# Two changes of order in a tuned attention and MoE kernel: when one block is transposed, and when the last chunk's own scores are made

## Chip, cores and metric

One NeuronCore of a Trainium2 chip. The metric is the device time of one launch, in microseconds (us), lower is better. The kernel is bound by TensorE (PE) almost throughout, so that this study is about a few us out of 1188.

## The reference, cut to what matters

```python
scores = (1.0 / S) * np.matmul(z, z.transpose(0, 2, 1))   # z: (8, 3008, 64)
attn   = np.maximum(scores, 0.0) ** 2
x      = u * np.matmul(attn, v)                           # u, v: (8, 3008, 256)
h      = x.reshape(-1, 256) @ w_in                        # (256, 2048)
out    = (h * (1.0 / (1.0 + np.exp(-1.702 * h)))) @ w_out # (2048, 256)
```

The scores are symmetric: block (i, c) is the transpose of block (c, i). The kernel makes most blocks only once and lets the DMA engines transpose ("turn") them for the other use.

## The kernel before

A batch of 3008 rows has six chunks of up to 512 rows. `attend(b, i)` multiplies chunk i's squared scores with v, in 47 or so steps ("slots"). A "unit" (i, jp) is a pair of 128-row blocks of scores; ScalarE rectifies it and VectorE squares it into a tile `a`. In the first batch, blocks are turned in the order of a list:

```python
ORDER0 = [(0, 1), (0, 2), (1, 2), (0, 3), (1, 3), (0, 4), (2, 3), (1, 4), (2, 4), (3, 4)]

def turn_unit(b, i, jp, a):            # two of these make one block (i, jp // 2)
    ...
    sp.dma_start_transpose(TT[b, i, cj][:, k0:k0 + 2]..., a...)
```

Block (2, 3) is chunk 2's, turned for chunk 3. All turning goes through SyncE's one queue, in program order. Chunk 4 of the first batch then reads all blocks for one half of the channels (`c`), then for the other:

```python
elif i == full(b):                     # chunk 4, all batches but the last
    order = [[(c, FULL, j)] for c in cs for j in js]
    ...
else:                                  # two 64-row tiles at a time, swapped at half of the chunk
    order = [[(0, TOP, j), (1, LOW, j)] for j in js] + [half] + [[(1, TOP, j), (0, LOW, j)] for j in js]
```

At half of such a chunk the row tiles swap their PSUM banks; the first matmul after it waits for a GpSimd instruction that waits for the last one before it (`post` and `behind`, line 86: "the handshake"). At which slot new scores are made is a schedule. That of the last batch:

```python
SCHED_LAST = SCHED | {3: {n: 1 for n in (14, 34)} | {NJ: 2}, 4: {NJ: 2}, 5: {}}   # NJ = 24
```

So the last two units, chunk 5's own, (5,10) and (5,11), are made in slot 24 of chunk 4, and chunk 5's very first step reads their tile `al`, most of which is made from (5,10) by two DMA transposes (line 277).

## Time and profile before

| | before |
|---|---|
| median of the first comparison, 6 executions | 1188.24 us (1187.31 to 1188.84) |
| span of the profiled execution, TensorE busy | 1186.5 us, 1176.8 us |
| wait at 54.14 us, turned block (2,3), first batch | 1.84 us |
| wait at 1092.77 us, block `al`, last batch | 1.83 us |

TensorE's timeline of the kernel before has the two waits in brackets (start, duration, engine, line, operation, what ended the idle time):

```profile
55.98 0.82 PE L358 MATMUL o<-tt,V 64*128 64x512 f16 x6 [1.84 <-DMA tt<-a]
...
1094.60 0.37 PE L358 MATMUL o<-al,V 64*128 64x448 f16 x2 [1.83 <-DMA al<-a]
```

The page's row for the matmuls that read turned blocks (busy us, mean ns | idle before, releaser) has no other wait:

```profile
L358 PE MATMUL o<-tt,V 64*128 64x512 f16 (+1 forms) x1510 | 232.1, 377 | 1.8 <-DMA tt<-a 1.8
```

The handshake at half of chunk 4 of the last batch, in the timeline of weight loads:

```profile
1087.62 0.76 PEld L358 LDWEIGHTS <-V 64*128 64x128 f16 x10 [0.17 <-POOLq L86]
```

### The profile page before, as it was taken

What the parts mean: (1) busy time and instruction counts of PE and PEld (TensorE: products, weight loads), DVE (VectorE), ACT (ScalarE), POOL (GpSimd) and SP (SyncE); (2) the same over time, 40 slices, a digit from 0 to 9 for tenths busy, and PEclk for the clock granted to TensorE, in tenths of its full rate; (3) what the DMA queues carried; (4) which work ended last, traced back from release to release, by engine and by line L of the source; (5) the groups of instructions that cost most, each with busy time, mean ns of one, the idle gap of its engine ahead of it and who ended that gap; (6) DMA issues with size and microseconds to landing.
All of it is one profiled execution on the core that took longest, in us unless ns stands there. A gap on an engine that the chain in (4) does not pass through costs nothing.

```text
span 1186.5 us, 27918 instructions
## 1 busy us (share of the span) xinstructions
PE 1176.8 (99%) x11526; PEld 699.6 (59%) x11526; DVE 837.7 (71%) x1441; ACT 819.3 (69%) x997; POOL 226.6 (19%) x319
## 2 busy tenths in 40 slices
PE   9999999999999999999999999999999999999998
PEld 3446764467644676447754478544784457844577
DVE  6688865877758776587775877658786487763776
ACT  7778864688646887478764787657866578672785
POOL 5243101231012310133101430014200241001000
PEclk9999999999999999999999999999999999999999
DMA  9998677866787677855789457895558875694012
GB/s 218 162 146 134 124 146 133 85 110 135 141 135 84 108 151 144 134 78 95 157 146 133 78 94 153 158 115 96 114 126 167 109 97 105 143 163 90 1 37 73
DMA packets 378880, 142.88 MB, mean 120 GB/s; under 512 B 320032, under 2 KB 372640, under 8 KB 378752
## 3 DMA queue, kind: packets, MB, share of 16 engines
q1 hardware_dynamic: 320464, 99.39, 46.3%
q0 software_dynamic: 56768, 40.39, 23.5%
q8 instruction: 90, 1.47, 0.5%
q10 hardware_dynamic: 1520, 1.31, 0.3%
q14 instruction: 38, 0.31, 0.1%
HBM read 60.29 MB, written 24.64 MB: 72 GB/s over the span
## 4 chain that ended last, share of the span: by engine, by line
PE 96%; ACT 1%; DMA 1%; issue 1%; DVE 1%; SPq 0%; DVEq 0%; ACTq 0%
PE o L358 39%; PE hg L399 27%; PE st L518 24%; PE sc L235 5%; ACT rl L256 1%; DMA tt<-a 1%; PE yp L493 1%; DMA al<-a 0%; PE w L99 0%; DVE a L270 0%; ACT ZT L143 0%; SPq L277 0%; DVE ut L202 0%; ACT gf L407 0%; DVE WT L446 0%
## 5 line engine op out<-in xcount | busy, mean ns | idle before, releaser
L407 ACT ACTIVATE gf<-hg 128x1024 f32<-128x1024 f32 (+1 forms) x384 | 385.5, 1004 | 143.7 <-PE hg L399 121.4
L256 ACT ACTIVATE rl<-sc 128x1024 f16<-128x1024 f32 (+1 forms) x301 | 287.7, 993 | 153.7 <-PE sc L235 108.4
L358 PEld LDWEIGHTS <-V 64*128 64x128 f16 (+1 forms) x4052 | 218.0, 95 | 257.9 <-issue 16.3
L399 PE MATMUL hg<-xt,W 128*128 128x512 f16 (+1 forms) x1408 | 354.6, 374 | 0.0
L411 DVE TENSOR_SCALAR gt<-gf 128x1024 f16<-128x1024 f32 (+1 forms) x320 | 222.9, 697 | 137.2 <-ACT gf L407 134.5
L358 PE MATMUL o<-a,V 64*128 64x512 f16 (+3 forms) x2240 | 296.1, 368 | 0.2 <-DVE a L270 0.2
L270 DVE TENSOR_TENSOR a<-rl 128x1024 f16<-128x1024 f16 (+1 forms) x266 | 178.5, 675 | 123.3 <-ACT rl L256 122.6
L195 POOL DMA_DIRECT2D uq<-in_u_dram x188 | 127.8, 687 | 692.0 <-PE sc L235 456.4
L358 PE MATMUL o<-tt,V 64*128 64x512 f16 (+1 forms) x1510 | 232.1, 377 | 1.8 <-DMA tt<-a 1.8
L399 PEld LDWEIGHTS <-W 128*128 128x128 f16 x1536 | 139.3, 98 | 119.2 <-issue 2.6
L518 PEld LDWEIGHTS <-gt 128*128 128x128 f16 x2944 | 177.1, 98 | 32.2
L518 PEld LDWEIGHTS <-s 128*128 128x128 f16 x2208 | 133.7, 98 | 25.6 <-issue 0.5
L235 PE MATMUL sc<-ZT 64*128 64x512 f16 (+3 forms) x688 | 114.6, 356 | 0.7 <-ACT ZT L143 0.4
L518 PE MATMUL st<-WT,gt 128*128 128x128 f16 x1472 | 97.8, 219 | 0.0
L518 PE MATMUL st<-WT,s 128*128 128x128 f16 x1472 | 96.6, 219 | 0.2 <-ACT uP L530 0.2
L518 PE MATMUL st<-W,gt 128*128 128x128 f16 x1472 | 96.6, 219 | 0.0
L536 DVE SCALAR_TENSOR_TENSOR y<-st,uP 128x256 f32<-128x256 f32 (+1 forms) x144 | 57.9, 409 | 28.3 <-ACT uP L530 19.9
L530 ACT ACTIVATE uP<-st 128x256 f32<-128x256 f32 (+1 forms) x144 | 53.0, 368 | 31.5 <-DVE y L536 16.2
L375 DVE TENSOR_TENSOR xt<-o,ut 128x512 f16<-128x512 f32 x80 | 51.4, 684 | 27.6 <-PE o L358 27.6
L409 ACT ACTIVATE gt<-gf 128x1024 f16<-128x1024 f32 (+1 forms) x64 | 65.9, 1030 | 2.1
L474 DVE TENSOR_TENSOR s<-s,gt 128x1024 f16<-128x1024 f16 (+1 forms) x96 | 64.4, 671 | 1.1
L472 DVE TENSOR_TENSOR s<-gt 128x1024 f16<-128x1024 f16 (+1 forms) x96 | 64.8, 675 | 0.0
(53 smaller groups left out, 600.2 us busy)
## 6 DMA issues: line engine op xcount, KB each, us to landing
out_dram<-y SPq DMA_DIRECT2D x40, 512.0 KB, 3.6
uq<-in_u_dram POOLq DMA_DIRECT2D x156, 128.0 KB, 3.7
V<-in_v_dram POOLq DMA_DIRECT2D x35, 256.0 KB, 6.4
tt<-a SPq DMA_TRANSPOSE x232, 3.9
uq<-in_u_dram POOLq DMA_DIRECT2D x32, 112.0 KB, 4.6
out_dram<-y SPq DMA_DIRECT2D x7, 384.0 KB, 3.1
vst<-in_v_dram SPq DMA_DIRECT2D x3, 512.0 KB, 5.9
zst<-in_z_dram POOLq DMA_DIRECT2D x7, 192.0 KB, 8.4
```

The costliest lines, as they stand in the source:

```text
L195: eng.dma_start(uq[k * QW:(k + 1) * QW, :n // QW].rearrange("t q c k -> t q (c k)"), src[:, :, cs])
L235: pe.matmul(sc[:, r, :q1 - q0], zt[h, 2 * kp + r, :], zt[h].rearrange("d n p -> d (n p)")[:, q0:q1], start=True, stop=True,)
L256: act.activation(rl[:, :, :n], sc[:, :, :n], AF.Relu, scale=csc)
L270: dve.tensor_tensor(a[:, :, :n], rl[:, :, :n], rl[:, :, :n], ALU.mult)
L358: ins = pe.matmul(acc[c][:, :n], V16[b][h, j].rearrange("p (c k) -> p k c", k=NCC)[:, c], weights(b, i, j)[h], start=(k, m) == first[c], s ...
L399: pe.matmul(hg[:, e, :n], W1[:, c, ff * P:(ff + 1) * P], XT[b, i][:, c, :n], start=(c == 0), stop=(c == NCC - 1),)
L407: act.activation(gf[:, :, :n], hg[:, :, :n], AF.Gelu_apprx_sigmoid, scale=1.0 / FSC)
L409: act.activation(g, gf[:, :, :n], AF.Copy, scale=FSC)
L411: dve.tensor_scalar(g, gf[:, :, :n], FSC, None, ALU.mult)
L472: dve.tensor_tensor(s_, a21, a22, ALU.add)
L474: dve.tensor_tensor(s_, ST[b, k, "S1", h], a11, ALU.subtract)
L518: pe.matmul(bank[:, m, :], lhs()[:, f, m, :], right[:, ff, :], start=name in ("P1", "P2", "P5") and m == 0 and ff == 0, stop=ff == NFF // ...
```

## The change

Its intent is to take away both waits: (2,3) is turned one place earlier, and chunk 5's own units are made 22 slots earlier.

```diff
-    ORDER0 = [(0, 1), (0, 2), (1, 2), (0, 3), (1, 3), (0, 4), (2, 3), (1, 4), (2, 4), (3, 4)]
+    ORDER0 = [(0, 1), (0, 2), (1, 2), (0, 3), (1, 3), (2, 3), (0, 4), (1, 4), (2, 4), (3, 4)]
-    SCHED_LAST = SCHED | {3: {n: 1 for n in (14, 34)} | {NJ: 2}, 4: {NJ: 2}, 5: {}}
+    SCHED_LAST = SCHED | {3: {n: 1 for n in (14, 34)} | {NJ: 2}, 4: {2: 2}, 5: {}}
```

Below, "part A" is the order and "part B" the slot.

## The prediction

> **What bounds the kernel now.** I read the page first. Its engine row and the head of its chain of work say that TensorE sets the time nearly everywhere:
>
> ```profile
> PE 1176.8 (99%) x11526; PEld 699.6 (59%) x11526; DVE 837.7 (71%) x1441; ACT 819.3 (69%) x997; POOL 226.6 (19%) x319
> ...
> PE 96%; ACT 1%; DMA 1%; issue 1%; DVE 1%; SPq 0%; DVEq 0%; ACTq 0%
> ```
>
> Only 1186.5 - 1176.8 = 9.7 us of the span are without a matmul in the array, and part of that is the start and the last store. The change adds and removes no instruction, so all it can win lies in these 9.7 us. The second view is therefore TensorE's list of waits (who was waited for: total us, times, longest us):
>
> ```profile
> PE o L358 <- DMA tt<-a: 1.8, 1, 1.8
> PE o L358 <- DMA al<-a: 1.8, 1, 1.8
> PE w L99 <- DVE nil L75: 1.2, 1, 1.2
> ```
>
> Two single waits of 1.8 us are in reach: one for a transposed block `tt`, one for the last chunk's own block `al`. The timeline places them: 54.14 us (first batch, chunk 3) and 1092.77 us (last batch, first matmul of chunk 5). Everything between runs on TensorE without another wait over 0.2 us.
>
> The chain of work around the first one:
>
> ```profile
> 47.23 0.69 DVE a L270 x2
> 47.92 8.02 DMA tt<-a
> 55.94 0.04 issue
> 55.98 0.82 PE o L358 x6
> ```
>
> The transpose issued at 47.92 needed 8.02 us to land. The DVE row ahead of it is a coincidence: the program order shows that this is the second transpose of block (2,3), chunk 2 for chunk 3. Its data were squared in chunk 1's last slots, done at about 37.3 us (the second of two 0.69 us squares at 35.70 and 36.62). What held it is SyncE's own queue, which issues one transpose behind the other from 24.94 to 65.3 us with no pause over 0.15 us. Read one by one, its landings are: (1,3) 42.0 and 45.8, (0,4) 48.2 and 49.8, (2,3) 50.9 and 55.9, (1,4) 57.5 and 59.1, (2,4) 61.7 and 62.4, (3,4) 69.3 and 71.5 us.
>
> The chain around the second wait:
>
> ```profile
> 1087.51 0.21 PE sc L235 x2
> 1087.72 0.02 issue
> 1087.74 0.93 ACT rl L256
> ...
> 1089.51 1.18 SPq L277
> 1090.69 0.05 issue
> 1090.74 3.72 DMA al<-a
> 1094.46 0.14 issue
> 1094.60 0.66 PE o L358 x3
> ```
>
> This is latency, not load: scores at 1087.5, rectified, squared, two transposes, landing at 1094.46, while ScalarE had been idle for 7.26 us before it.
>
> **What the Trainium skill says.** "TensorE: Matmul & The Clock Gate", section "Back-to-back issue gap", gives N/2.4 + 2.5 ns between warm matmuls, 216 ns for N=512; here the pairs on two row tiles start at 1086.486, 1086.702 and 1086.918, so 0.216 us apart, while each is drawn 0.376 us long. A gap read between bars thus understates a stall. "TensorEngine Tiling (Array Packing)", "Gotcha 1: PSUM Pressure", says row tiles cannot access one PSUM bank at the same time and software has to synchronize; the kernel does this at half of a chunk with a GpSimd semaphore instruction, visible as a PEld wait at L86. "DMA: Bandwidth & Descriptors", "Queues, rings and completion order", says each DMA engine goes round-robin between queue rows by packets; from 66 to 70 us the software queue had 1462 packets and the hardware queue 1468, so it agrees. "Perfetto Trace Analysis", "DMA Instruction — HWDGE (DVE, Sync)", says that the reported span of such an instruction leaves out the movement; here issues of 1.2 to 5.3 us landed 3.2 to 11.3 us after their start.
>
> **Part A, the order of turning.** The two transposes of (2,3) change places with the two of (0,4); the order of all engines else is unchanged. Data of (2,3) are ready (37.3) before the earlier pair was issued (38.90), so nothing new holds the queue. (2,3) should land at about 48.2 and 49.8, and TensorE wants it at 54. The wait ends with 4 us to spare. What it cost: the last matmul before it started at 53.784 (448 columns, 0.19 us pitch), so the next was due at 53.975 and came at 55.979: 2.00 us, not 1.84. (0,4) now lands at 50.9 and 55.9; chunk 4 first reads it at 65.92 - 2.0 = 63.9. The buffers that (0,4) frees are next written some 10 us later; the program order moves that semaphore wait to squares at about 58 us. Both harmless.
>
> What is not free is the next deadline. Block (3,4), the last of the queue for chunk 4, landed at 71.51. Chunk 4's step 16 reads it, the third matmul of this row, so at 72.40 + 2 x 0.216 = 72.83:
>
> ```profile
> 72.40 0.81 PE L358 MATMUL o<-tt,V 128*128 128x512 f16 x3
> ```
>
> With TensorE 2.0 us earlier it wants (3,4) at 70.83. The DMA share in these stretches (window, its length, then busy time by engine; the last two columns are clock and DMA share with GB/s) is over one all the way:
>
> ```profile
> 38.00:54.00 16.00, 16.00 (x152) 7.25 (x147) 12.04 (x20) 13.72 (x15) 3.40 (x6) 1.00 1.22 138
> 54.00:56.00 2.00, 0.16 (x4) 0.02 (x3) 1.33 (x3) 1.01 (x2) 0.00 (x0) 1.00 1.14 146
> 56.00:73.00 17.00, 17.00 (x119) 8.43 (x119) 10.28 (x17) 13.47 (x15) 4.78 (x6) 1.00 1.35 192
> ```
>
> So the queue is bound by throughput and will not follow TensorE. If (3,4) lands where it did, a new wait of 71.51 + 0.04 - 70.83 = 0.72 us appears. GpSimd's weight loads and the next batch's z load start 2.0 us earlier too, as they wait for the half of chunk 3 (58.67 before); these are in front of (3,4) in both kernels, so finishing them earlier may bring it forward, by up to about 1 us as I judge it. I take a new wait of 0.4 us, between 0 and 0.8. Part A: 2.0 - 0.4 = 1.6 us.
>
> **Part B, the own units of chunk 5.** Four score matmuls move from slot 24 of chunk 4 to slot 2, about 1082.2 us. PSUM is free (last rectification ended at 1080.5), ScalarE idle, VectorE busy with the two gates until 1083.7; then square, transposes from about 1084.5 and, at the 3.7 to 4.0 us that the old ones took to land, data by about 1089. Needed at 1092.9. Without the wait: last matmul 1092.386, next due 1092.60, came at 1094.595, so 1.99 us.
>
> But slot 24 is where TensorE waits for the GpSimd handshake, and the moved matmuls covered it. Last matmul of the first half: start 1087.137, end 1087.513; GpSimd answers at 1087.555; TensorE goes on at 1087.627. With nothing in between it was due at 1087.349. So 0.28 us of it comes into the open. The 0.27 us of scores are paid in slot 2 instead. Part B: 1.99 - 0.28 = 1.71 us.
>
> **Sum.** 1.6 + 1.7 = 3.3 us. From the first wait on TensorE is the bound, so the shift should reach the end: 1187.97 - 3.3 = 1184.7 us, a ratio of 1.003.
>
> **Rivals.** (1) The queue keeps (3,4) back for the whole 0.72 us or, with loads mixing differently, longer, up to eating all of part A: for it speaks the DMA share over one, against it that loads ahead of it finish earlier. Time 1185.0 to 1186.3. (2) Waits vanish and nothing takes their place, the handshake being hidden by weight loads pulled ahead: 1187.97 - 4.0 = 1184.0. Against it: the weight load itself waits for the handshake, 0.17 us in the old trace even with cover. (3) VectorE and ScalarE, nearly on the path at 91 to 102 us (their rows are in the chain there), take back some of it: but that stretch starts from a TensorE score at 90.83 us and should shift as a whole; I give at most 0.3 us.
>
> **Range and chances.** All rivals lie between 1184.0 and 1186.3; three runs of before spread over 0.8 us. I take 1183.9 to 1186.0. Two per cent are 23.8 us, more than all idle time of TensorE, so faster by that is excluded; slower by that would need a stall that the program order doesn't show.
>
> **What would show it.** Right: no TensorE wait for `tt` near 54 us, none for `al` near 1090; (2,3) landed before 51 us; a short wait for `tt` near 71 us; a PEld wait at L86 near 1085 us of about 0.25 us where it was 0.17. Wrong: a first (2,3) transpose that starts after 40 us, a `tt` wait over 1 us at 71, a TensorE matmul count busy for longer than 1176.8 us by more than 1 us, or another wait in chunk 5 of the first batch that takes back what chunk 3 won.

## The result and the profile after

Ratios are the mean time of one kernel's runs over that of the other's of the same rounds, so not quite the ratio of the medians.

| | before | after |
|---|---|---|
| first comparison, median | 1188.24 us | 1185.74 us |
| lowest and highest of 6 | 1187.31, 1188.84 | 1184.62, 1191.08 |
| ratio, 95% interval | | 0.9988 (0.9968 to 1.0009) |
| span of the profiled execution | 1186.5 us | 1187.0 us |

The median fell by 2.5 us, but the ratio says only 1.4 us, because two of six executions took 1188.79 and 1191.08 us. By luck the profile is of the first of these, 4 us over the fastest. It shows what went wrong there. Its list of TensorE's waits, and the page's row:

```profile
PE o L358 <- DMA tt<-a: 3.6, 2, 3.1
```

```profile
L358 PE MATMUL o<-tt,V 64*128 64x512 f16 (+1 forms) x1510 | 232.3, 377 | 3.8 <-DMA tt<-a 3.6
```

The wait for `al` is gone. The wait for a turned block has not gone but moved, and grown from 1.8 to 3.6 us in two pieces. TensorE's timeline places them:

```profile
69.95 0.61 PE L358 MATMUL o<-tt,V 128*128 128x512 f16 x2 [0.54 <-DMA tt<-a]
...
77.60 0.38 PE L358 MATMUL o<-tt,V 128*128 128x512 f16 x1 [3.10 <-DMA tt<-a]
```

There is none at 54 us: (2,3) landed at 50.9 and 53.1 us, and the matmul that waited before has no bracket:

```profile
54.13 0.81 PE L358 MATMUL o<-tt,V 64*128 64x512 f16 x6
```

Block (2,4) landed at 69.9 instead of 62.4 us, and (4,5), the last of the queue, at 77.56 instead of 73.28 us. The chain of that execution at the second piece:

```profile
71.09 6.47 DMA tt<-a
77.56 0.04 issue
77.60 0.38 PE o L358
```

But this execution's queue was already late before the change could act. Up to (1,3) both kernels issue the same transposes in the same order, and the second transpose of (1,3) landed at 49.25 us here, at 45.84 us in the profile of before. So the DMA engines don't take the same time in two executions, and one profile of each kernel doesn't say what the order does.

In the last batch the profile answers without doubt. The two transposes of `al` go out at 1086.95, and the matmul that reads it follows its predecessor without a wait; the handshake, with nothing to cover it, shows 0.61 us of idle weight loading in place of 0.17:

```profile
1086.95 2.46 SPq L277 DMA_TRANSPOSE al<-a  x2
...
1095.06 0.35 PE L358 MATMUL o<-al,V 64*128 64x448 f16 x2
```

```profile
1090.08 4.86 PEld L358 LDWEIGHTS <-V 64*128 64x128 f16 x48 [0.61 <-POOLq L86]
```

The 0.61 us counts from the end of a weight load. What TensorE lost is read from starts: the last matmul of the first half began at 1089.589, the next was due 0.212 later, at 1089.80, and began at 1090.082: 0.28 us.

Because the instructions of TensorE are the same in all these kernels from the first batch's end to the last batch, whole stretches can be compared by start times of the same matmul. From the 10500th to the 10700th matmul record (last batch, chunk 4 into 5) the kernel before took 31.74 us and the changed one 30.01 us. Part B is worth 1.73 us here. The experiments below repeat this: the stretch took 30.01 us in every one of the fourteen profiles that have part B, and 31.74 to 33.60 us in the five that have the old slot (before, e1, g3, h1, h4).

### The profile page after: what moved, and what is told of

Its sections match the earlier page's. It is cut to its first block, busy times and chain, and to the rows that moved or that the text cites. A ratio compares the mean times of both kernels' runs of the same rounds, so it can differ in the third digit from the quotient of the medians.

```text
span 1187.0 us, 27920 instructions
## 1 busy us (share of the span) xinstructions
PE 1177.2 (99%) x11526; PEld 698.5 (59%) x11526; DVE 837.1 (71%) x1441; ACT 819.8 (69%) x997; POOL 226.0 (19%) x319
## 4 chain that ended last, share of the span: by engine, by line
PE 97%; ACT 1%; DVE 1%; DMA 1%; issue 0%; DVEq 0%; ACTq 0%; POOLq 0%
PE o L358 39%; PE hg L399 27%; PE st L518 24%; PE sc L235 6%; PE yp L493 1%; DMA tt<-a 1%; ACT rl L256 1%; PE w L99 0%; ACT gf L407 0%; DVE a L270 0%; DVE ut L202 0%; ACT ZT L143 0%; PE zp L135 0%; DVE zst L128 0%; DVE WT L446 0%
## 5 line engine op out<-in xcount | busy, mean ns | idle before, releaser
L530 ACT ACTIVATE uP<-st 128x256 f32<-128x256 f32 (+1 forms) x144 | 53.1, 368 | 31.7 <-DVE y L536 15.6
```

## The experiments

Two theories after the result. **C**: the moved wait is the change's doing, TensorE comes 2 us sooner to the last turned blocks while the next batch's z load is under way. **L**: the turning queue is late by itself in some executions, and either order pays for it somewhere. Five groups followed, eighteen kernels, each group on one chip with the kernel before in the same rounds. All gave correct results.

### Each part alone, the change again, and the z load held

`e1_order_only` has the first line of the diff alone, `e2_slot_only` the second alone, `e3_both_again` is the change. `e4_hold_z` is the change with one line more, which makes GpSimd read block (4,5) before it issues the second half of the next batch's z load:

```diff
+            if b == 1 and n0: pool.tensor_copy(const.tile([P, 1], F16, name="hold2"), TT[0, NCH - 2, NCH - 1][:, 2, 0, :1])
```

> The first part alone: (2,3) turned in front of (0,4); the last batch as before. Theory C (collision): the wait of 2.0 us at 54 us goes, but from 69 to 77 us TensorE waits for the last turned blocks (3,4) or (4,5), because it reaches them 2 us sooner while the second half of the next batch's z load shares the DMA engines with them; loss there 0 to 5 us, different from execution to execution, so the mean is within 1 us of before and the times spread by over 3 us. Rival P (as predicted): one new wait of at most 0.8 us, 1.2 to 2.0 us faster than before, spread under 2 us. In both the wait for the last chunk's own block near 1092 us stays at 1.8 us.

> The second part alone: own units of chunk 5 in slot 2 of chunk 4; the first batch as before. Both theories: no wait near 1093 us, 0.28 us lost at the handshake in slot 24, so 1.7 us faster than before (1.4 to 2.0), with the spread of before (about 1.5 us). The wait of 1.8 us near 54 us stays. If the second part were the cause of the wide spread, the times here would spread by over 4 us.

> The change again, unaltered, for a second profile and five more times. Theory C: times spread by over 3 us again, some at 1184.6 and some over 1187; in the profile the waits near 70 to 77 us add up to the profiled time less 1184.3. Rival Q (the first profile was an outlier of the measurement): times within 1.5 us of 1185.

> The change, and in the first batch GpSimd reads one column of block (4,5) before it issues the second half of the next batch's z load, so that this load cannot be under way while the last turned blocks land. Theory C: no wait of over 1 us at 74 us, mean 1184.3 to 1185.3, about 3.3 us faster than before, spread under 2 us. Rival L (the hardware queue is late by itself in some executions, whatever the z load does): spread over 3 us as with the change, and waits for turned blocks of 1 to 5 us near 70 to 77 us in slow executions.

| | median us | all executions | ratio to before (1187.40) |
|---|---|---|---|
| e1_order_only | 1187.42 | 1186.77 to 1188.69 | 1.0000 (0.9988 to 1.0012) |
| e2_slot_only | 1185.76 | 1185.20 to 1186.10, one 1189.34 | 0.9989 (0.9977 to 1.0001) |
| e3_both_again | 1185.51 | 1185.09 to 1185.56 | 0.9980 (0.9968 to 0.9992) |
| e4_hold_z | 1186.96 | 1184.64 to 1192.72, three over 1187.9 | 1.0008 (0.9988 to 1.0028) |

The order alone wins nothing that shows: its interval is 1.4 us wide to each side. The slot alone wins 1.64 us in the median, and both together 1.89 us. The profile of the slot alone says why. It has the old order, and the list of TensorE's waits begins

```profile
PE w L99 <- DVE nil L75: 1.2, 1, 1.2
PE sc L235 <- ACT ZT L143: 0.3, 1, 0.3
```

with no wait for a turned block at all: (2,3) landed at 47.86 us and was due at 54.5. In the profile of the order alone the only wait over 1.2 us is that for `al`:

```profile
PE o L358 <- DMA al<-a: 1.9, 1, 1.9
```

So the 2.0 us at 54 us in the first profile were one execution's, not the kernel's. Theory C fails as the general cause: both e1 and e3 run the new order without a wait in chunk 4, and the five executions of e3 lie within 0.5 us, where C expected over 3. e4 missed its expectation: its profiled execution was a fast one without waits, but three of its six were slow, and none of these was profiled. Holding the z load does not tame the spread, and whether it makes it worse is open.

### Chunk 4 relaxed, and a queue made late on purpose

`g1_pairs_both` is the change with chunk 4 of the first batch read block by block for both channel halves, which moves the first use of the last blocks back, by 8 us as the expectation has it (in g1's profile (3,4) is first read at 80.9 us and (4,5) at 85.2, which is 9.5 and 11.2 us later than half by half); `g2_pairs_slot_only` the same with the old order.

```diff
-            order = [[(c, FULL, j)] for c in cs for j in js]
+            order = [[(c, FULL, j)] for j in js for c in cs] if b == 0 else [[(c, FULL, j)] for c in cs for j in js]
```

`g3_before_delayed` and `g4_after_delayed` are the two kernels with four extra loads at the load of u for chunk 2:

```diff
+            if (b, i) == (0, 2): eng.dma_start(W1[k * QW:(k + 1) * QW, 0, :1024].rearrange("t (q x) -> t q x", q=16), src[:, :, cs])
```

> The change, and chunk 4 of the first batch goes block by block, each block for both halves of the channels, in place of all blocks for one half and then for the other. This puts the first use of (3,4) from about 71 to about 79 us and of (4,5) from about 74 to about 82 us, at no cost in matmuls. Theory L (the turning queue is late by a few us in some executions and the change only moves the wait to the last blocks of chunk 4): no wait for a turned block over 0.3 us, times 1184.6 to 1185.6 in all executions, spread under 1.2 us. Rival S (the wide spread comes with the moved units of the last batch, whatever chunk 4 does): some executions 3 us or more over the fastest.

> As the run before, but with the old order of turning ((0,4) in front of (2,3)). What is left to differ is the wait for (2,3) near 54 us alone. Theory L: nothing to win in executions with an early queue (1184.6 to 1185.6), 1 to 6 us lost in those with a late one, so a mean 0.3 to 1.5 us above the run before and a wider spread. If the order never matters on this chip, both are the same within 0.3 us.

> The kernel before, with four more loads of 128 KB (data that nothing reads, into a weight tile that is not loaded yet) on GpSimd's queue at about 20 us: it makes the turning queue late on purpose, by 2 to 4 us. Theory L: the wait for (2,3) near 54 us grows to 2 to 6 us, waits in chunk 4 stay under 1 us, time 2 to 5 us above before. Against L: no wait at 54 us and no change in time.

> The change with the same four extra loads. Theory L: at most 1 us of wait near 54 us, but 2 to 5 us of waits for (2,4), (3,4) or (4,5) between 69 and 78 us, so that the order of turning wins less than 1.5 us of what the delay costs the kernel before: time 1187 to 1190. Against L: waits gone in both places and 1185.

| | median us | all executions | ratio to before (1187.45) |
|---|---|---|---|
| g1_pairs_both | 1185.49 | 1185.12 to 1185.60, one 1190.29 | 0.9986 (0.9971 to 1.0001) |
| g2_pairs_slot_only | 1185.25 | 1185.04 to 1186.92 | 0.9981 (0.9969 to 0.9993) |
| g3_before_delayed | 1188.14 | 1187.26 to 1188.81, one 1194.98 | 1.0015 (0.9991 to 1.0038) |
| g4_after_delayed | 1185.56 | 1185.27 to 1185.69 | 0.9980 (0.9965 to 0.9994) |

512 KB more were not enough: in g3 (2,3) landed at 49.7 us, and no turned block was waited for in g3 or g4. The order makes no difference between g1 and g2 either. One slow execution in g1 (1190.29), which the relaxed chunk 4 should have excluded, suggests that not all slow executions come from chunk 4's deadlines; it was not profiled.

g3's profile gave something else. Its wait for `al` was 2.12 us long, and after it the granted clock fell to half. The windows of its profile, cut at the edges of the clock record (start and end, length, then busy time and instructions of TensorE, weight loads, VectorE, ScalarE, GpSimd, then clock, DMA share, GB/s):

```profile
1089.74:1093.16 3.42, 1.41 (x14) 0.43 (x10) 1.29 (x2) 0.00 (x0) 0.00 (x0) 1.00 0.37 90
1093.16:1096.57 3.41, 3.30 (x10) 1.19 (x11) 0.00 (x0) 0.52 (x1) 0.00 (x0) 0.50 0.00 0
1096.57:1099.98 3.41, 3.41 (x18) 1.66 (x17) 1.39 (x2) 2.45 (x3) 0.00 (x0) 1.00 0.00 0
```

A window of 3.41 us in which TensorE idled 3.42 - 1.41 = 2.0 us is followed by one at clock 0.50, in which 10 matmuls were issued in place of 18. In the profile of before the same wait lay otherwise in its window and no drop followed:

```profile
1092.83:1096.24 3.41, 1.65 (x9) 0.82 (x10) 1.27 (x2) 0.08 (x1) 0.00 (x0) 1.00 0.02 5
1096.24:1099.65 3.41, 3.41 (x19) 1.59 (x18) 1.39 (x2) 2.78 (x3) 0.00 (x0) 1.00 0.00 0
```

The stretch that took 31.74 us in that profile took 33.60 us in g3's. Of these 1.86 us the longer wait is 0.3 us, so that the drop itself costs about 1.6 us. This also fits the two clusters in the times of the kernel before. In the five groups it was executed 45 times with its clock recorded: 28 took at most 1187.7 us, all with a mean clock of 0.999 or 1.000; 17 took 1188.5 us or more, 13 of them with 0.998. Half clock for 3.41 of 1187 us is 0.0014 of the mean, and the medians of the 28 and of the 13 lie 1.66 us apart. A comparison that no run was made for supports it. With the wait in place and no extra loads (before, e1 and i4, 55 executions) 15 have a clock of 0.998 and a time between 1188.4 and 1189.9 us. Of the 51 executions of kernels with part B (without e4, j1 and j2) none has both; the two at 0.998 took over 1190 us.

### Later loads, and the load that collides

Four extra loads behind the load of u for chunk 3 (about 37 us) in all four: `h1_before_late` on the kernel before, `h2_after_late` on the change, `h3_pairs_late` on g1, `h4_before_late_u4` as h1 with u for chunk 4 loaded at about 59 instead of 47.6 us.

```diff
+        for k in range(P // QW if (b, i) == (0, 3) else 0): eng.dma_start(W1[k * QW:(k + 1) * QW, 0, :1024].rearrange(...), src[:, :, k * NCC * QW:(k + 1) * NCC * QW])
```
```diff
-    LOAD0 = {(1, 14): 2, (2, 12): 3, (2, NJ + 20): 4, (4, 8): 5}
+    LOAD0 = {(1, 14): 2, (2, 12): 3, (3, NJ + 20): 4, (4, 8): 5}
```

> The kernel before, with four more loads of 128 KB on GpSimd's queue right behind the load of u for chunk 3 (issued at about 37 us; data that nothing reads). Theory M: a transpose that is issued after the load of u for chunk 4 (about 47.6 us) shares the DMA engines with it and lands 5 to 8 us later instead of 2 to 4. Here the second transpose of (2,3) slips behind 47.6 us, so it lands at 55 to 60 us and TensorE waits 1.5 to 6 us near 54 us. Against M: it lands before 54 us, no wait.

> The change with the same loads. Theory M: (2,3) goes two places ahead of the slip and lands before 54 us; no wait there or under 1 us. The queue stays late, so waits of 0.5 to 4 us for (2,4), (3,4) or (4,5) between 69 and 78 us; it wins 0 to 3 us over the run before in the first 100 us. Rival: no wait in either place, then the order wins the whole wait of the run before.

> The change, chunk 4 block by block for both halves, and the same loads. Theory M: no wait for a turned block of over 0.3 us anywhere in the first batch, times within 1 us of 1185.4.

> As the first run of this call (old order, extra loads), but the load of u for chunk 4 stands behind the weight loads, at about 59 us. Theory M: the second transpose of (2,3) lands within 4 us of its issue, before 54 us, so the wait near 54 us is gone although the order is the old one. Against M (the queue is late by itself): the wait stays at 1.5 to 6 us.

| | median us | all executions | ratio to before (1188.58) |
|---|---|---|---|
| h1_before_late | 1190.73 | 1188.78 to 1197.37 | 1.0029 (0.9997 to 1.0061) |
| h2_after_late | 1185.49 | 1185.27 to 1186.76 | 0.9977 (0.9962 to 0.9992) |
| h3_pairs_late | 1185.36 | 1185.07 to 1185.75 | 0.9974 (0.9959 to 0.9989) |
| h4_before_late_u4 | 1192.34 | 1189.13 to 1195.77 | 1.0042 (1.0011 to 1.0072) |

h1's expectation failed: (2,3) still landed in time, at 50.73 us, and nothing waited for it. (No turned block was waited for in h2 and h3 either.) What its profile shows is a weight load that came late,

```profile
PE hg L399 <- DMA W<-in_moe_w_in_dram: 2.7, 1, 2.7
```

and, again, a clock drop after it:

```profile
65.76:69.17 3.41, 0.75 (x4) 0.40 (x5) 0.75 (x2) 0.62 (x1) 0.00 (x0) 1.00 1.34 153
69.18:72.59 3.41, 3.41 (x10) 1.22 (x8) 0.69 (x1) 1.02 (x1) 0.00 (x0) 0.50 1.65 135
```

h4 bears on what makes (2,3) late. Its second transpose was issued at 48.33 us, later than in the first profile (47.92), but with the load of u for chunk 4 out of the way it landed 4.0 us after its issue, not 8.0, and there was no wait at 54 us. The traffic was only moved, though: two waits of together 1.4 us for the last turned blocks came up at 71 and 75 us:

```profile
PE o L358 <- DMA tt<-a: 1.4, 2, 1.0
```

In h3, (4,5) landed at 76.78 us. Read half by half, chunk 4 would have wanted it at about 73.8 us (73.42, from before's 75.42 less the 2.0 us wait, and 0.33 us later start of this execution); read block by block it waited for nothing. By this estimate the relaxed chunk 4 saved about 3 us here, in an execution with a late queue; it is the one place where it shows.

### Eight and twelve extra loads, and another slot

`i1_old_order_later` (e2 as base), `i2_new_order_later` (the change) and `i3_pairs_later` (g1) have the extra loads behind u for chunks 2 and 3, now into a part of `W2`, which is loaded much later. `i4_slot20` is the kernel before with one number changed:

```diff
-    SCHED_LAST = ... 4: {NJ: 2}, 5: {}}
+    SCHED_LAST = ... 4: {20: 2}, 5: {}}
```

> Old order of turning, moved units of the last batch, and eight more loads of 128 KB (four behind the load of u for chunk 2, four behind that for chunk 3; data that nothing reads). Theory M: the second transpose of (2,3) is issued after 48 us, lands at 54 to 60 us, and TensorE waits 1 to 6 us near 54 us; times 1186.5 to 1191.

> The change with the same eight loads. Theory M: (2,3) is issued before 48 us and lands before 54.5 us, no wait or under 1 us there; waits for (2,4), (3,4) or (4,5) of 1 to 5 us between 66 and 78 us; time 0 to 3 us below the run before. If it is more than 4 us below, the order is worth its whole wait; if it is above, the order costs time in late executions.

> The change with chunk 4 block by block for both halves, and the same eight loads. Theory M: the waits between 66 and 78 us of the run before are gone or under 0.5 us; times 1185.0 to 1186.5.

> The kernel before, with the own units of chunk 5 in slot 20 of chunk 4 in place of 24: four slots of 0.216 us sooner, so the wait near 1092 us shrinks from 1.8 to 2.1 us to 1.0 to 1.3, and 0.28 us is lost at the handshake. Theory H (a window of 3.41 us with 2.0 us idle or more halves TensorE's clock for the next one, 1.7 us lost): no execution in the upper cluster by this cause, times 1186.2 to 1187.0, clock 0.999 to 1.000. Rival: the two clusters have another cause, then they stay, 0.6 us below those of before.

| | median us | all executions | ratio to before (1187.31) |
|---|---|---|---|
| i1_old_order_later | 1185.81 | 1185.44 to 1186.11, one 1191.66 | 0.9996 (0.9975 to 1.0016) |
| i2_new_order_later | 1185.52 | 1185.05 to 1185.66 | 0.9981 (0.9967 to 0.9995) |
| i3_pairs_later | 1185.41 | 1185.03 to 1186.11 | 0.9982 (0.9968 to 0.9995) |
| i4_slot20 | 1187.43 | 1187.00 to 1187.85, one 1190.67 | 1.0005 (0.9992 to 1.0019) |

Again (2,3) did not slip: issued at 46.99 us in i1, landed at 50.78. No turned block was waited for in the three profiles, in either order.

i4 missed as well, and usefully. Made four slots earlier, the units saved nothing: the wait for `al` is still 1.74 us, and the stretch is 31.92 us against 31.74. Its chain ends with

```profile
1088.86 4.12 DMA al<-a
```

and the time from issue to landing of `al`'s two transposes (shortest, median, longest) in i4, then in before, then in the slot alone is

```profile
DMA to landing us min/median/max: 4.1/4.8/5.5
```
```profile
DMA to landing us min/median/max: 3.7/3.9/4.0
```
```profile
DMA to landing us min/median/max: 2.3/2.7/3.0
```

At half of chunk 4, right behind the handshake, GpSimd issues the load of u for chunk 5. In i4 these loads go out at 1086.91 us and the transposes at 1086.99, into the middle of them; in before the loads were issued a little ahead (1088.31 against 1089.51); in the slot alone the transposes landed by 1087.57, when the loads, issued from 1087.13, had not moved a packet yet. So part B wins by two things, the earlier start and a free set of DMA engines, and four slots give only a part of the first while they make the second worse (one profile of each kernel). As a test of the clock theory i4 is void, since the wait did not shrink; what speaks for that theory is the comparison above.

A last pair, `j1_old_order_latest` and `j2_new_order_latest`, had twelve extra loads behind u for chunk 3 (`range(12 if (b, i) == (0, 3) else 0)`), on e2 and on the change.

> Old order, moved units of the last batch, twelve more loads of 128 KB behind the load of u for chunk 3 (issued from about 37 to 45 us; data that nothing reads). Theory M: second transpose of (2,3) issued after 48 us and landed at 55 to 62 us, TensorE waits 1 to 7 us near 54 us; time 1187 to 1193.

> The change with the same twelve loads. Theory M: (2,3) lands before 55 us, wait there under 1 us; the queue stays late, so (2,4), (3,4) or (4,5) cost 1 to 6 us between 66 and 78 us. The order then wins the difference of the two sums, expected 0 to 3 us; the rival is that it wins the whole first wait (no wait in chunk 4).

They took 1193.01 us (1191.73 to 1194.63; ratio 1.0042, 1.0027 to 1.0057) and 1191.67 us (1191.15 to 1193.90; 1.0035, 1.0018 to 1.0052), but not for the reason expected. The waits of j1, then of j2:

```profile
PE o L358 <- POOLq L86: 5.8, 1, 5.8
```
```profile
PE o L358 <- POOLq L86: 4.7, 1, 4.7
```

GpSimd was still issuing the extra loads when TensorE came to the handshake at half of chunk 2, at 44 us (in j1 with pauses of 1.3 and 1.9 us, each ended by the landing of an earlier load), and TensorE stood still until GpSimd got to it. Half clock followed, for 6.8 us in j1 and 3.4 us in j2. After that long a stop, TensorE was late enough for every turned block: in j1 (2,3) did slip, to 56.41 us, but TensorE, which would have wanted it at about 54.5 us, came to it at 62.8. The pair says nothing of the order.

## Why the prediction was right or wrong

The predicted median, 1184.7 us, was 1.0 us under the measured 1185.74, but the gain was forecast at 3.3 us and is 1.4 us by the first comparison's ratio and 2.4 us by e3's (0.998). That the median came so near is in part luck: 1.6 us of the forecast did not exist, and a cost that the prediction didn't know of, the clock drop, went away in its place. Two of its own signs of being wrong showed in the first profile: the first transpose of (2,3) started at 43.85 us, after 40, and a wait for `tt` was over 1 us (3.10, though near 74 and not at 71).

**Part A failed at its first step**: "so the next was due at 53.975 and came at 55.979: 2.00 us". The arithmetic holds for the execution that was profiled. The step took that execution's wait for the kernel's. Eight more profiles have the old order; in seven the first batch reached the place undisturbed (the eighth is j1, stopped earlier by the handshake):

| old order | second transpose of (2,3): issued, landed | due |
|---|---|---|
| before | 47.92, 55.94 | 53.98 |
| e2 | 43.20, 47.86 | 54.5 |
| g2 | 47.81, 53.37 | 54.2 |
| g3 | 45.89, 49.68 | 54.4 |
| h1 | 46.81, 50.73 | 54.1 |
| h4 (u for chunk 4 later) | 48.33, 52.30 | 54.4 |
| i1 | 46.99, 50.78 | 54.7 |
| i4 | 42.45, 46.52 | 54.3 |

"Due" is 53.98 plus the later start of each execution. One in eight waited, although four of these carried extra traffic. The times agree: of the 45 executions of the kernel before in the five groups at most five leave room for a wait of 2 us, the four over 1188.5 us without the low clock and the one at 1189.84. (The 28 of the lower cluster lie within 1.0 us, and the other 12 of the upper one are above it by no more than the clock drop.) Part A measured 0 (ratio 1.0000, 0.9988 to 1.0012) where 1.6 us were put down, and beside part B the two orders differ by 0.3 us or less in the median: e3 is 0.25 us under e2, g1 0.24 over g2, i2 0.29 under i1. Its mechanism is right as far as it goes: the new order lands (2,3) two places sooner and no profile of it waits at 54 us. There was mostly nothing to win.

**The rival "the queue keeps (3,4) back"** is the nearest to the slow executions of the first comparison, but named the wrong block. In the profiled one, (2,4) cost 0.54 us and (4,5) 3.10 us, (3,4) nothing. The prediction took (3,4) for the last of the queue for chunk 4, worked out its slack, and not that of the block behind it: (4,5) landed at 73.28 us before, and is wanted at 75.42 - 2.0 = 73.4 once the first wait is gone. That is 0.1 us of slack, on a queue whose landings differ by several us between executions.

**Part B was right in size**: 1.71 us predicted, 1.73 us between the same two matmuls in the traces, with the handshake's 0.28 us to the hundredth, and 1.64 us in the median of the slot alone. Two things in it were not foreseen. The transposes land in 2.3 and 3.0 us, not in the 3.7 to 4.0 that the prediction carried over, because the u load no longer runs against them. And the wait sometimes cost twice its length: where it left TensorE idle for 2.0 us of a clock window, a window at half clock followed and cost about 1.6 us more. With the wait gone this is gone, and the mean gain of part B can be above its own sum: it is 2.3 to 2.4 us by the ratios of g2, e3 and g4, where no execution was slow, and 1.3 us by that of e2, with one at 1189.34. The step "1.99 - 0.28 = 1.71 us" lacks that term for 13 of 45 executions by the clock. As the half clock lies in TensorE's busy time, the bound "all it can win lies in these 9.7 us" was not strict either.

**The sum** therefore should have been 0 + 1.7 us, plus 0 or about 1.6 us for the clock, not 1.6 + 1.7. The shift did reach the end undiminished, as said: from the end of the first batch's attention to the last batch the matmuls of before and after keep the same distance to within 0.02 us.

**What stays open.** The rare slow executions, 3 us or more over the rest, are not all explained. The profiled one (1188.79 us) is explained by its late turned blocks. The others, 1191.08 of the change and single ones of e2, g1, g3, i1 and i4, three of e4, one of h1 and two of h4, were not profiled. Late turned blocks, a late weight load (h1) and a late handshake (j1) each can do it, as single profiles show; which of them did is not known. They do not fall evenly on the two orders. With extra loads (j1 and j2 left out) 6 of 16 executions with the old order took over 1190 us (g3, h1, h4, i1) and none of 20 with the new; h1's median lies 5.2 us over h2's, of which part B accounts for 1.7 us, or 3.3 with a clock drop. Without extra loads it is 2 of 66 with the old order and 4 of 28 with the new. That the order works on these rare executions, either way, is thus a rival to "worth nothing" which no profile settles.

Nor is it shown what the order of turning is worth when (2,3) truly slips: of four attempts to force this three (g3, h1, i1) did not, and in j1 the handshake hid it. That a load of u for chunk 4 under way is what makes it slip is supported by h4 (4.0 against 8.0 us to land), a single execution. Other profiles fit: in e1 to e4 and g1 the transposes issued from 44 to 47.4 us landed after 3.3 to 5.0 us, and those issued from 47.4 to 51 us, about with that load (47.7 to 48.2 us) or behind it, after 5.1 to 10.8 us. A weight load follows 2 to 3 us later, so that the two are not told apart.

No version beats the change by more than the noise: with chunk 4 read block by block the median of 14 executions is 1185.41 us, without it that of 23 executions of the change is 1185.49, both with and without extra loads.

## What to carry to other kernels

A wait seen in one profile is one sample. Before paying for its removal, look whether it stands in a second execution, above all if it ends on a transfer in a stretch where the DMA share is over one; the wait for `al`, at the end of a chain of latencies, was there in all six profiles with the units in slot 24 or 20 (1.74 to 2.25 us). When a wait is taken away, work out the slack of every later deadline of the same queue, not only of the next one. And when work moves away from a handshake, price the handshake; when a transfer moves, look at what else is in flight at its new time.

## What the Trainium skill lacked or had wrong

- "TensorE: Matmul & The Clock Gate", section "What's actually happening", puts the return to the slow clock after at least one idle window of about 3.4 us. Here windows of 3.41 us with 2.0 us (g3) and 2.7 us (h1) of idle TensorE were followed by a window at clock 0.50, while windows with 1.76 us (before) and 1.95 us (the profile after) were not. All twenty traces, cut into windows of 3.413 us from the first edge of their clock records, agree: each of the 17 windows with 2.0 us or more of idle TensorE, ends of kernels included, was followed by half clock, and none with 1.95 us or less. So here a window that is idle for three fifths is enough, and a wait's place in the window decides: in h1 a wait of 2.25 us for `al`, longer than g3's 2.12, fell on two windows (0.9 and 1.3 us idle) and no drop followed. The window's length agrees (3.413 us in the clock record).

```profile
75.65:79.06 3.41, 1.46 (x7) 0.68 (x7) 1.02 (x2) 0.19 (x1) 1.13 (x2) 1.00 1.10 162
79.06:82.47 3.41, 3.41 (x17) 1.57 (x16) 2.32 (x4) 2.65 (x3) 3.41 (x6) 1.00 0.79 123
```

- "TensorEngine Tiling (Array Packing)", "Gotcha 1: PSUM Pressure", asks for synchronization between row tiles and gives no price. Through another engine it cost 0.28 us when bare, nothing when 0.27 us of other matmuls stood in front of it, and 4.7 and 5.8 us when that engine was held up issuing loads (j2, j1).
- "DMA: Bandwidth & Descriptors", "Queues, rings and completion order", tells that queues share the engines but not what this does to a DMA transpose: 2.3 to 3.0 us from issue to landing with no load beside it, 4.1 to 5.5 us against four loads of 112 KB.
- No page that I read says how far DMA timing differs between executions of one program: the second transpose of (1,3), with the same instructions ahead of it, landed at 45.84 us in one profile and at 49.25 us in another.
